# A hand-planned order: transposes, block sums, softmax subtractions and weight mixing at other places of the time table

## The chip, the cores and the metric

One core of one Trainium2 chip. The metric is device time in microseconds; the kernel before was run three times, and one further execution was taken with the hardware profiler. The work runs on five engines with a queue each: PE (TensorE: matrix products into PSUM), DVE (VectorE), ACT (ScalarE), POOL (GpSimd) and SP (SyncE, which issues the transfers). Each engine works off its queue strictly in order; an instruction whose input is not ready, or whose output buffer is not free, holds up all that stands behind it on its engine.

## The reference

Attention within chunks of 64 positions, then a product with the largest of three projections:

```python
B, H, S, D, chunk = 8, 8, 576, 64, 64
scores = scale * np.matmul(q_c, k_c.transpose(0, 1, 2, 4, 3))    # (8, 8, 9, 64, 64)
scores = scores - np.max(scores, axis=-1, keepdims=True)
attn = np.exp(scores)
attn = attn / (np.sum(attn, axis=-1, keepdims=True) + 1e-09)
out = np.matmul(attn, v_c)
x = out.transpose(0, 2, 1, 3).reshape(4608, 512)
h = np.maximum(np.maximum(x @ w1, x @ w2), x @ w3)               # each w: 512 x 768
return h @ w_out                                                 # 768 x 512
```

All of it is fp32.

## The kernel before

**Tiles and units.** The 4608 tokens are 36 tiles of 128. Eight tiles (two groups of four) go through the products plainly; the other 28 are four units of 7, 8, 7 and 6 tiles, whose products are computed by blocks with seven products in place of eight (`ORDER`, `OUTER` give their order). Each fp32 factor is split into a high and a low part, so each product is three matmuls (lines 173 to 176 for the groups, `product`, line 584, for the units).

**One tile** goes through: scores `S` (PE, L227), maximum `mx` (DVE, L232), subtraction `sub` (DVE, L237), `exp` (ACT, L241), `sum`, `eps`, `rec` (DVE, L182, L185, L188), the scaling `nrm` (L191, on DVE for the first tiles, on POOL for the later ones), the transpose `T` (PE, L253), its copy `at` (ACT, L258), the product with the values `V` (PE, L265) and the copy `x` into the staging tile (ACT, L279).

**One unit.** First its operands: sums of blocks `mix` (L496; numbers 5 and 6 on DVE, 7 and 4 on POOL), `high` parts (ACT, L501) and `low` parts (DVE, L505). Then nine sets (`hidden`: three column blocks jp by three weights w), each with the seven products of `ORDER` (1, 6, 5, 2, 7, 3, 4). Products 1, 6 and 5 are copied out of PSUM by ACT (L598) after which 2, 7 and 3 accumulate in the same banks (`banks_of_product`); DVE adds products 7, 3 and 4 to kept blocks (L601) and takes the maximum (L595), POOL adds two more (L604, L608). After the last weight of a column block seven operands Y are made for the second product: t5 and t6 on DVE (L638, L626), t7 and t4 on POOL (L638), high parts on ACT (L631), low parts on DVE (L634). Then `project` multiplies Y with w_out: copies on ACT (L675), sums on DVE (L678) and POOL (L681), stores. Block sums of the weights are made meanwhile (`store` L370 to L405, `store_out` L426 to L461).

**What sets the order.** The order of each engine's queue is written by hand. The start is a list of names, `FIRST`. From there on a planner writes it: `plan(at, pe, fn)` puts a piece of work into a heap under a due time, and each step of the PE's main work advances a clock and lets out what has come due, in the order of due times:

```python
    def passed(step):
        nonlocal now
        now += step
        while due and due[0][0] <= now:
            _, _, pe, fn = heapq.heappop(due)
            fn()
            now += pe
```

The numbers in `SOFTMAX`, in `operands_behind`, in the `after` lists of `hidden` and `project`, in `tiles` and `transposes` are such due times in us, relative to a step of PE. They change nothing but the place at which an instruction stands in its engine's queue; at run time nothing waits for them, only for data and buffers.

Of the kernel before, what the change touches and what calls it, by code (L numbers as in the profile page):

```python
# [64 lines left out]
def chunk_attn_maxout_kernel(  # L65
# [223 lines left out]
    def moe(t0, x_of, banks_in=((ps_m, "pm"),)):  # L289
# [50 lines left out]
        def project(*tts, before=JT - 1):  # L340

            for js in (range(before), range(before, JT)):
                for tt in tts:
                    for j in js:
                        onto(tt, j)
                        yield [(0.3, lambda tt=tt: output(tt))] if j == JT - 1 else []

        def hidden(j, w):
            for ct, _ in enumerate(products(j, w, 0, 512)):
                yield [] if ct < CT - 1 else [(0.3, lambda: maximum(j, w, 0, 512))] + (  # L350
                [(1.1, lambda: high(j, 0, 512)), (1.8, lambda: low(j, 0, 512))] if w == 2 else [])
# [8 lines left out]
    def store(n):  # L360
# [42 lines left out]
        def mixed():  # L403
            for k in range(2):
# [13 lines left out]
    def store_out(jp):  # L418
# [41 lines left out]
        def mixed():  # L460
# [4 lines left out]
        return [(0.0, whole(0)), (2.1, whole(1)), (3.5, originals), (4.2, sum_of(2, a21, a22, plus, True)),  # L465
                (5.9, sum_of(0, sums(2), a11, minus)), (7.6, sum_of(1, a11, a21, minus)),
                (9.3, sum_of(3, a12, sums(0), minus)), (12.0, high), (13.4, low), (17.0, mixed)]
# [3 lines left out]
    def unit(t0, count, rooms):  # L471
# [35 lines left out]
        def operands():  # L507
            return [(0.0, high(1)), (1.2, low(1)), (2.4, mix(5, b12, b11, nc.vector)), (3.4, high(5)),
                    (3.6, mix(6, b22, source[5], nc.vector)), (4.6, mix(7, b22, b12, nc.gpsimd)), (4.8, high(6)),
                    (5.8, low(6)), (5.9, high(2)), (7.0, low(5)), (8.0, mix(4, b21, source[6], nc.gpsimd)), (8.2, low(2)),  # L510
                    (8.3, high(7)), (9.4, low(7))]

        def operands_behind():

            return [(0.1, high(1)), (1.3, low(1)), (2.5, mix(5, b12, b11, nc.vector)), (2.5, mix(7, b22, b12, nc.gpsimd)),
                    (3.6, mix(6, b22, source[5], nc.vector)), (4.4, high(5)), (5.5, low(5)), (6.3, high(6)),
                    (6.7, mix(4, b21, source[6], nc.gpsimd)), (7.2, high(2)), (7.4, low(6)), (8.2, high(7)), (8.5, low(2)),
                    (9.7, low(7))]
# [68 lines left out]
        def hidden(n, loads):  # L587
# [18 lines left out]
            after = {1: [(0.25, copy(1, 0))], 5: [(0.25, copy(5, 1))],  # L606
                     6: [(0.25, copy(6, 2)),
                         (0.95, lambda: nc.gpsimd.tensor_tensor(out=kept(2), in0=kept(2), in1=kept(0), op=plus))],  # L608
                     7: [(0.25, sum_to(7, 0, lambda: kept(3))), (1.0, fourth)],
                     3: [(0.25, sum_to(3, 2, lambda: o[3] if w else M(0, 1)))],  # L610
# [3 lines left out]
            else:  # L614
                after[2] = [(0.25, greater(0, 0, lambda: o[2]))]
                after[7].append((2.2, greater(1, 1, lambda: kept(1))))
                after[3].append((0.95, greater(0, 1, lambda: o[3])))
                after[4].append((0.95, greater(1, 0, lambda: o[4])))
            if w == 2:
# [17 lines left out]
                def less(eng, out, x, y):  # L637
# [18 lines left out]
        def project(loads):  # L656
# [3 lines left out]
            def store(m, name, make):  # L660
# [11 lines left out]
                return [(0.25, fn), (1.0, out)]  # L672
# [10 lines left out]
            for p, i in enumerate(OUTER):  # L683
                for m in range(2):
                    after = {1: lambda: [(0.25, copy(m, 1, 0))],
                             2: lambda: store(m, (0, 0), lambda out, m=m: nc.scalar.copy(out=out, in_=o[m][2])),
                             6: lambda: [(0.25, copy(m, 6, 2)), (0.95, second(m))],
                             7: lambda: [(0.25, lambda m=m: sum_of(m, 7, 0)(kept(m)))],
# [3 lines left out]
                    if m:  # L692
                        after += [(0.3, fn) for fn in loads[p]]
# [145 lines left out]
    def first_tiles(time):  # L839
        gap = (time - 8.0) / 8  # L840
        for n in range(UNITS[0] + 2):
            at = now + 7.0 + gap * n
            insert(at, (("V", n - 2), ("S", n)))
            softmax(n, at, nc.vector if n < UNITS[0] else nc.gpsimd)
            if n < UNITS[0] + 1:
                insert(at + 9.2, (("T", n),))
                plan(at + 9.6, 0.0, lambda n=n: steps(n)["at"]())
            if n < UNITS[0]:
                plan(at + 0.5, 0.0, lambda n=n: steps(n)["v"]())
            if n > 1:  # L850
                plan(at + 1.0, 0.0, lambda n=n: steps(n - 2)["x"]())
# [163 lines left out]
```

## Time and profile before

| what | us |
|---|---|
| three runs | 631.44, 632.88, 632.89 (median 632.88) |
| profiled execution, whole | 632.87 |
| its span on the core | 631.1 |
| PE busy in the span | 615.1 (97%) |
| DVE, ACT, POOL busy | 445.7 (71%), 272.0 (43%), 278.6 (44%) |

Times in the trace are us from the span's start. A PE row of the timeline with xcount n is n matmuls back to back; its bracket is the idle time ahead of it and the instruction whose end released it. A group's busy time is not its time on the clock: matmuls overlap.

### The profile page before, as it was taken

To read this page: it belongs to the slowest core of one execution; us is meant where nothing else is said; L and a number is where in the kernel's file an instruction comes from. 1 tells how busy PE (TensorE), PEld (TensorE's weight loads), DVE (VectorE), ACT (ScalarE), POOL (GpSimd) and SP (SyncE) were. 2 spreads that over 40 slices of the span, in tenths; PEclk is the share of its full clock that TensorE was granted. 3 is DMA by queue.
4 is the path that set the end of the run, shared out by engine and by line. 5 is a ranking of instruction groups with operands and counts; after the bars stand their busy time and mean duration, and the time that the engine had idled before them with its cause. 6 is when DMAs were issued, how large, how long until landed. Compare 5 with 4: busy or idle time off the path is not lost.

```text
span 631.1 us, 12694 instructions
## 1 busy us (share of the span) xinstructions
PE 615.1 (97%) x5102; PEld 533.7 (85%) x5102; DVE 445.7 (71%) x684; ACT 272.0 (43%) x483; POOL 278.6 (44%) x235
## 2 busy tenths in 40 slices
PE   7899999999999999999999999989999999999997
PEld 3788887887889888888887888778999899999997
DVE  4898964788756879589559585985476758466752
ACT  4887634345544534353434342533252335232340
POOL 2422577765446864336325252352343535143430
PEclk9999999999999999999999999989999999999999
DMA  8978558575789998475967574748956756987774
GB/s 331 370 286 302 197 184 342 200 277 186 307 258 338 343 343 328 135 267 175 404 224 249 169 260 157 259 160 298 335 178 193 246 160 221 356 290 258 235 226 174
DMA packets 54220, 161.26 MB, mean 256 GB/s; under 512 B 4881, under 2 KB 17169, under 8 KB 49169
## 3 DMA queue, kind: packets, MB, share of 16 engines
q1 hardware_dynamic: 54160, 160.45, 71.8%
q8 instruction: 40, 0.66, 0.4%
q14 instruction: 20, 0.16, 0.1%
HBM read 128.97 MB, written 31.46 MB: 254 GB/s over the span
## 4 chain that ended last, share of the span: by engine, by line
PE 73%; DVE 18%; ACT 3%; issue 3%; POOL 2%; DVEq 0%; POOLq 0%; ACTq 0%
PE pm L584 52%; PE pm L174 5%; PE pm L175 5%; PE pm L176 5%; DVE Y L634 4%; DVE e L237 2%; DVE mx L232 1%; DVE sm L182 1%; PE s L265 1%; PE s L227 1%; DVE most L595 1%; DVE sm L185 1%; DVE s L391 1%; DVE X L505 1%; ACT e L241 1%
## 5 line engine op out<-in xcount | busy, mean ns | idle before, releaser
L584 PE MATMUL pm<-X,ring 128*128 128x448 f32 (+2 forms) x1512 | 313.6, 366 | 3.4 <-DVE most L601 2.0
L584 PEld LDWEIGHTS pm<-X,ring 128*128 128x128 f32 x1512 | 276.2, 188 | 31.9 <-DVE most L601 4.2
L598 ACT COPY kept<-pm 128x448 f32<-128x448 f32 (+2 forms) x108 | 57.4, 534 | 142.9 <-PE pm L584 118.6
L584 PE MATMUL pm<-Y,ring 128*128 128x448 f32 (+2 forms) x504 | 106.5, 370 | 1.0 <-DVE kept L678 0.4
L584 PEld LDWEIGHTS pm<-Y,ring 128*128 128x128 f32 x504 | 93.2, 190 | 11.4 <-DVE Y L634 1.1
L595 DVE TENSOR_TENSOR most<-pm,most 128x448 f32<-128x448 f32 (+2 forms) x72 | 44.8, 622 | 53.3 <-PE pm L584 51.9
L608 POOL TENSOR_TENSOR kept<-kept 128x448 f32<-128x448 f32 (+2 forms) x36 | 45.0, 1251 | 72.8 <-ACT kept L598 72.8
L634 DVE TENSOR_TENSOR Y<-most,Y 128x448 fp32r<-128x448 f32 (+2 forms) x72 | 58.0, 822 | 12.1 <-ACT Y L631 12.0
L174 PE MATMUL pm<-xh,wl 128*128 128x512 f32 (+1 forms) x156 | 60.8, 390 | 0.0
L175 PE MATMUL pm<-xl,wh 128*128 128x512 f32 (+1 forms) x156 | 58.4, 374 | 0.3 <-DVE xl L276 0.3
L176 PE MATMUL pm<-xh,wh 128*128 128x512 f32 (+1 forms) x156 | 58.4, 375 | 0.0
L191 POOL TENSOR_TENSOR e<-e,sm 128x512 f32<-128x512 f32 x26 | 28.7, 1104 | 61.1 <-DVE sm L188 60.2
L604 POOL TENSOR_TENSOR kept<-kept 128x448 f32<-128x448 f32 (+2 forms) x24 | 31.0, 1292 | 55.4 <-DVE kept L601 55.4
L631 ACT CAST Y<-most 128x448 fp32r<-128x448 f32 (+2 forms) x72 | 40.1, 568 | 22.4 <-DVE most L595 15.3
L601 DVE TENSOR_TENSOR kept<-pm,kept 128x448 f32<-128x448 f32 (+2 forms) x36 | 22.3, 620 | 22.2 <-PE pm L584 10.8
L241 ACT ACTIVATE e<-e 128x512 f32<-128x512 f32 x36 | 22.8, 633 | 33.6 <-DVE e L237 33.4
L601 DVE TENSOR_TENSOR pm<-pm,kept 128x448 f32<-128x448 f32 (+2 forms) x48 | 30.1, 628 | 5.6 <-PE pm L584 5.3
L176 PEld LDWEIGHTS pm<-xh,wh 128*128 128x128 f32 x156 | 29.3, 188 | 5.5
L174 PEld LDWEIGHTS pm<-xh,wl 128*128 128x128 f32 x156 | 29.3, 188 | 5.5
L175 PEld LDWEIGHTS pm<-xl,wh 128*128 128x128 f32 x156 | 29.4, 189 | 5.2 <-DVE xl L276 0.5
L232 DVE TENSOR_REDUCE mx<-s 128x8 f32<-128x512 f32 x27 | 18.4, 683 | 20.8 <-ACT stage L279 12.1
L182 DVE TENSOR_REDUCE sm<-e 128x8 f32<-128x512 f32 x36 | 24.5, 681 | 7.1 <-ACT e L241 6.6
(111 smaller groups left out, 852.2 us busy)
## 6 DMA issues: line engine op xcount, KB each, us to landing
ring<-w SPq DMA_DIRECT2D x36, 1024.0 KB, 5.2
ring<-w SPq DMA_DIRECT2D x36, 768.0 KB, 4.6
ring<-wo SPq DMA_DIRECT2D x28, 768.0 KB, 4.6
buf<-in_qk SPq DMA_DIRECT2D x36, 512.0 KB, 6.0
buf<-in_vb SPq DMA_DIRECT2D x36, 256.0 KB, 4.9
w<-s SPq DMA_DIRECT2D x18, 512.0 KB, 4.4
stage<-in_w SPq DMA_DIRECT2D x7, 512.0 KB, 4.6
out_t<-ao SPq DMA_DIRECT2D x16, 224.0 KB, 6.1
```

The costliest lines, as they stand in the source:

```text
L174: nc.tensor.matmul(out=o, lhsT=al, rhs=bh, start=first, stop=False)
L175: nc.tensor.matmul(out=o, lhsT=ah, rhs=bl, start=False, stop=False)
L176: nc.tensor.matmul(out=o, lhsT=ah, rhs=bh, start=False, stop=last)
L182: nc.vector.tensor_reduce(out=sm, in_=e, axis=AX.X, op=ALU.add)
L584: nc.tensor.matmul(out=o[i], lhsT=a, rhs=b, start=new and k == 0, stop=last and k == 2, skip_group_check=i in banks_of_product)
L595: return lambda: nc.vector.tensor_tensor(out=M(k, c), in0=of(), in1=M(k, c), op=most)
L598: return lambda: nc.scalar.copy(out=kept(k), in_=o[i])
L601: return lambda: nc.vector.tensor_tensor(out=out(), in0=o[i], in1=kept(k), op=plus)
L604: nc.gpsimd.tensor_tensor(out=kept(1) if w else M(1, 1), in0=kept(3), in1=kept(1), op=plus)
L608: (0.95, lambda: nc.gpsimd.tensor_tensor(out=kept(2), in0=kept(2), in1=kept(0), op=plus))],
L631: return lambda: nc.scalar.copy(out=y_room(i, jp)[:, 0, :half], in_=t[i]())
L634: return lambda: nc.vector.tensor_tensor(out=y_room(i, jp)[:, 1, :half], in0=t[i](), in1=y_room(i, jp)[:, 0, :half].bitcast(F32), op=minus)
```

## The change

Only the planner's numbers change. Every engine has the same instructions as before, in another order from about 95 us on. The core of the diff:

```diff
-SOFTMAX = (("mx", 1.0), ("sub", 1.9), ("exp", 2.8), ("sum", 3.8), ("eps", 4.7), ("rec", 4.9), ("nrm", 5.3))
+SOFTMAX = (("mx", 1.12), ("sub", 1.12), ("exp", 2.8), ("sum", 3.8), ("eps", 4.7), ("rec", 4.9), ("nrm", 5.3))
-OPERANDS = 0.3
-MIX = 0.5
+OPERANDS = 0.28
+MIX = 0.19
...
         def operands_behind():
-            return [(0.1, high(1)), (1.3, low(1)), (2.5, mix(5, b12, b11, nc.vector)), (2.5, mix(7, b22, b12, nc.gpsimd)),
-                    (3.6, mix(6, b22, source[5], nc.vector)), (4.4, high(5)), (5.5, low(5)), (6.3, high(6)),
-                    (6.7, mix(4, b21, source[6], nc.gpsimd)), (7.2, high(2)), (7.4, low(6)), (8.2, high(7)), (8.5, low(2)),
+            return [(0.1, high(1)), (1.25, low(1)), (2.5, mix(5, b12, b11, nc.vector)), (2.5, mix(7, b22, b12, nc.gpsimd)),
+                    (2.52, mix(6, b22, source[5], nc.vector)), (4.53, high(5)), (5.5, low(5)), (6.3, high(6)),
+                    (6.58, mix(4, b21, source[6], nc.gpsimd)), (7.48, high(2)), (6.48, low(6)), (8.2, high(7)), (9.66, low(2)),
                     (9.7, low(7))]
...
-            after = {1: [(0.25, copy(1, 0))], 5: [(0.25, copy(5, 1))],
-                     6: [(0.25, copy(6, 2)),
+            after = {1: [(0.33, copy(1, 0))], 5: [(0.69, copy(5, 1))],
+                     6: [(0.0, copy(6, 2)),
...
-                     7: [(0.25, sum_to(7, 0, lambda: kept(3))), (1.0, fourth)],
-                     3: [(0.25, sum_to(3, 2, lambda: o[3] if w else M(0, 1)))],
+                     7: [(0.11, sum_to(7, 0, lambda: kept(3))), (1.0, fourth)],
+                     3: [(0.0, sum_to(3, 2, lambda: o[3] if w else M(0, 1)))],
...
-                             (1.0, less(nc.gpsimd, t[7], lambda: M(1, 1), lambda: M(0, 1))), (1.6, t6), (1.9, high(5)),
-                             (2.6, low(5)), (3.0, high(2)), (3.6, low(2)),
+                             (1.13, less(nc.gpsimd, t[7], lambda: M(1, 1), lambda: M(0, 1))), (1.9, t6), (1.12, high(5)),
+                             (2.62, low(5)), (3.0, high(2)), (3.21, low(2)),
...
-                             (6.9 if last else 5.2 * f, high(3)), (7.5 if last else 5.9 * f, low(3)),
-                             (5.8 * f, high(7)), (6.5 * f, low(7)), (6.4 * f, high(6)), (7.1 * f, low(6)),
-                             (7.0 * f, high(4)), (7.7 * f, low(4))]
+                             (5.33 if last else 4.94 * f, high(3)), (7.5 if last else 6.07 * f, low(3)),
+                             (4.91 * f, high(7)), (6.62 * f, low(7)), (6.4 * f, high(6)), (7.46 * f, low(6)),
+                             (6.66 * f, high(4)), (7.57 * f, low(4))]
...
-                    after = {1: lambda: [(0.25, copy(m, 1, 0))],
+                    after = {1: lambda: [(0.85, copy(m, 1, 0))],
...
-                             7: lambda: [(0.25, lambda m=m: sum_of(m, 7, 0)(kept(m)))],
+                             7: lambda: [(2.0, lambda m=m: sum_of(m, 7, 0)(kept(m)))],
...
-            plan(at + 0.5, 0.0, lambda: steps(n)["at"]())
+            plan(at + 1.19, 0.0, lambda: steps(n)["at"]())
...
-                plan(at - 16.0 + 2.0 * k, 0.0, lambda n=n: steps(n)["v"]())
+                plan(at - 16.34 + 2.0 * k, 0.0, lambda n=n: steps(n)["v"]())
...
-                transposes(n, at + begin + 9.2)
+                transposes(n, at + begin + 10.83)
...
-        parts.append(("do", lambda u=u: operands(u + 1, 6.5)))
+        parts.append(("do", lambda u=u: operands(u + 1, 7.23)))
```

The sums of the weights' blocks (`store`, `store_out`), the first tiles, the loads of q and the ring's loads shift in the same way, by 0.02 to 2 us.

On PE, in the project part of the second unit (around 403 to 418 us), the first `L253` is the transpose of tile 22, the second that of tile 23, and `L265` is the values' product of tile 22. Before:

```order
L584 MATMUL pm<-Y,ring 128x512 x6
L253 MATMUL y<-ident,e 128x128 x4
L584 MATMUL pm<-Y,ring 128x512 x54
L253 MATMUL s<-ident,e 128x128 x4
L584 MATMUL pm<-Y,ring 128x512 x27
L265 MATMUL y<-xs,buf 64x64 x16
```

and now:

```order
L584 MATMUL pm<-Y,ring 128x512 x15
L253 MATMUL y<-ident,e 128x128 x4
L584 MATMUL pm<-Y,ring 128x512 x51
L253 MATMUL s<-ident,e 128x128 x4
L584 MATMUL pm<-Y,ring 128x512 x21
L265 MATMUL y<-xs,buf 64x64 x16
```

Both transposes have moved back, by nine and by six matmuls.

On POOL, at the same place, `L191` is the scaling of tile 23 and the first `L496` is mix 7:

```order
 L638 TENSOR_TENSOR most<-most 128x512
 L638 TENSOR_TENSOR most<-most,m 128x512
+L191 TENSOR_TENSOR e<-e,sm 128x512
 L496 TENSOR_TENSOR stage<-stage 128x2x448
-L191 TENSOR_TENSOR e<-e,sm 128x512
-L681 TENSOR_TENSOR kept<-kept 128x512
+L681 TENSOR_TENSOR kept<-kept 128x512 x2
 L496 TENSOR_TENSOR most<-stage,most 128x2x448
-L681 TENSOR_TENSOR kept<-kept 128x512
```

The scaling has changed places with mix 7, and mix 4 has gone behind the second sum of `project`.

On DVE, in the first unit's third set of the second column block (246 to 253 us), `L232`, `L237`, `L182`, `L185` are steps of tile 14, and the `L601` are the sums of products 7, 3 and 4. Before:

```order
L232 TENSOR_REDUCE mx<-y 128x2x4
L237 TENSOR_TENSOR e<-y,mx 128x2x4x64
L634 TENSOR_TENSOR Y<-most,Y 128x448 x2
L601 TENSOR_TENSOR kept<-pm,kept 128x448
L182 TENSOR_REDUCE sm<-e 128x8
L634 TENSOR_TENSOR Y<-m,Y 128x448
L185 TENSOR_SCALAR sm<-sm 128x8
L634 TENSOR_TENSOR Y<-most,Y 128x448
L601 TENSOR_TENSOR most<-pm,kept 128x448
L188 RECIPROCAL sm<-sm 128x8
L601 TENSOR_TENSOR most<-pm,kept 128x448
```

and now:

```order
L232 TENSOR_REDUCE mx<-y 128x2x4
L237 TENSOR_TENSOR e<-y,mx 128x2x4x64
L634 TENSOR_TENSOR Y<-most,Y 128x448
L601 TENSOR_TENSOR kept<-pm,kept 128x448
L634 TENSOR_TENSOR Y<-most,Y 128x448
L182 TENSOR_REDUCE sm<-e 128x8
L634 TENSOR_TENSOR Y<-m,Y 128x448
L601 TENSOR_TENSOR most<-pm,kept 128x448
L634 TENSOR_TENSOR Y<-most,Y 128x448
L185 TENSOR_SCALAR sm<-sm 128x8
L188 RECIPROCAL sm<-sm 128x8
L601 TENSOR_TENSOR most<-pm,kept 128x448
```

The sums of products 7 and 3 each stand one low part of Y earlier. The same two exchanges stand in the third unit (493 to 499 us).

## Rows read from the trace of the kernel before

**Rows 1.** The profile page, its first part (busy time, share of the span, instructions) and a group of its fifth part (xcount | busy, mean ns of one | idle time before them).

```profile
PE 615.1 (97%) x5102; PEld 533.7 (85%) x5102; DVE 445.7 (71%) x684; ACT 272.0 (43%) x483; POOL 278.6 (44%) x235
...
L584 PE MATMUL pm<-X,ring 128*128 128x448 f32 (+2 forms) x1512 | 313.6, 366 | 3.4 <-DVE most L601 2.0
```

**Rows 2.** Busy time by stretch (the stretch in us, its length, then for each engine the busy time with its count, PEclk, DMA share, GB/s).

```profile
0.00:27.00 27.00, 22.17 (x367) 14.31 (x367) 17.11 (x33) 16.24 (x28) 12.21 (x16) 1.00 0.91 340
...
205.00:256.00 51.00, 47.91 (x473) 42.48 (x472) 42.17 (x65) 23.54 (x44) 32.26 (x27) 1.00 0.88 320
...
620.00:631.10 11.10, 7.72 (x45) 7.40 (x43) 3.30 (x6) 0.00 (x0) 0.00 (x0) 1.00 0.30 111
```

**Rows 3.** What PE waited for from 100 us to the end: what waits <- what it waited for: us in total, times, the longest.

```profile
PE s L253 <- POOL e L191: 2.2, 1, 2.2
PE pm L584 <- DVE most L601: 2.0, 2, 1.5
PE pm L584 <- ACT kept L598: 1.2, 1, 1.2
PE pm L584 <- DVE kept L678: 0.4, 1, 0.4
PE pm L584 <- DVE Y L634: 0.4, 1, 0.4
PE s L265 <- ACT xs L258: 0.4, 1, 0.4
PE y L227 <- issue: 0.4, 1, 0.4
```

**Rows 4.** Timeline around 408 us (start, length, engine, line, operation, xcount, in brackets the idle time before and what ended it).

```profile
407.01 1.09 DVE L496 TENSOR_TENSOR most<-stage 128x896 f32<-128x896 f32 x1
408.19 2.12 POOL L496 TENSOR_TENSOR stage<-stage 128x896 f32<-128x896 f32 x1 [5.66 <-DVE sm L185]
408.22 0.20 DVE L188 RECIPROCAL sm<-sm 128x8 f32<-128x8 f32 x1
408.34 2.92 DVE L496 TENSOR_TENSOR most<-stage,most 128x896 f32<-128x896 f32 x1
410.27 1.89 POOL L191 TENSOR_TENSOR e<-e,sm 128x512 f32<-128x512 f32 x1
...
412.21 0.69 PE L253 MATMUL s<-ident,e 128*128 128x128 f32 x4 [2.23 <-POOL e L191]
```

**Rows 5.** Busy time by stretch, the five us that follow; columns as in rows 2.

```profile
412.20:417.20 5.00, 4.99 (x17) 4.03 (x18) 5.00 (x3) 2.68 (x5) 5.00 (x3) 0.66 0.18 71
```

**Rows 6.** Timeline from 214 to 225 us; columns as in rows 4.

```profile
214.65 1.23 DVE L448 TENSOR_TENSOR so<-c,so 128x1024 fp32r<-128x1024 f32 x1 [0.84 <-ACT so L445]
...
222.50 0.61 DVE L601 TENSOR_TENSOR most<-pm,kept 128x448 f32<-128x448 f32 x1
223.04 0.68 DVE L237 TENSOR_TENSOR e<-y,mx 128x512 f32<-128x512 f32 x1
223.75 0.63 ACT L241 ACTIVATE e<-e 128x512 f32<-128x512 f32 x1 [3.59 <-DVE e L237]
224.28 0.95 ACT L598 COPY kept<-pm 128x448 f32<-128x448 f32 x2
...
224.85 1.48 PE L584 MATMUL pm<-X,ring 128*128 128x448 f32 x6 [1.16 <-ACT kept L598]
```

**Rows 7.** Timeline from 248 to 253 us; columns as in rows 4.

```profile
248.73 0.62 DVE L634 TENSOR_TENSOR Y<-most,Y 128x448 fp32r<-128x448 f32 x1 [0.62 <-ACT Y L631]
...
250.40 1.29 DVE L634 TENSOR_TENSOR Y<-m,Y 128x448 fp32r<-128x448 f32 x1
251.69 0.61 DVE L634 TENSOR_TENSOR Y<-most,Y 128x448 fp32r<-128x448 f32 x1
252.23 0.61 DVE L601 TENSOR_TENSOR most<-pm,kept 128x448 f32<-128x448 f32 x1
...
252.90 1.48 PE L584 MATMUL pm<-X,ring 128*128 128x448 f32 x6 [1.46 <-DVE most L601]
```

**Rows 8.** Timeline from 274 to 296 us; columns as in rows 4.

```profile
275.88 0.57 DVE L634 TENSOR_TENSOR Y<-most,Y 128x448 fp32r<-128x448 f32 x1
276.50 3.16 PE L584 MATMUL pm<-Y,ring 128*128 128x448 f32 x14 [0.42 <-DVE Y L634]
...
291.28 3.40 DVE L505 TENSOR_TENSOR X<-stage,X 128x1024 fp32r<-128x1024 f32 x1
...
295.27 2.09 PE L584 MATMUL pm<-Y,ring 128*128 128x448 f32 x9 [0.43 <-DVE kept L678]
```

**Rows 9.** Timeline from 487 to 499 us; columns as in rows 4.

```profile
487.95 0.53 ACT L598 COPY kept<-pm 128x448 f32<-128x448 f32 x1 [3.02 <-DVE sm L185]
488.67 0.57 ACT L631 CAST Y<-most 128x448 fp32r<-128x448 f32 x1 [0.18 <-DVE most L638]
...
491.71 6.33 PE L584 MATMUL pm<-X,ring 128*128 128x448 f32 x30
...
496.41 1.58 DVE L634 TENSOR_TENSOR Y<-most,Y 128x448 fp32r<-128x448 f32 x1
497.91 1.14 DVE L601 TENSOR_TENSOR most<-pm,kept 128x448 f32<-128x448 f32 x2
498.58 1.70 PE L584 MATMUL pm<-X,ring 128*128 128x448 f32 x7 [0.53 <-DVE most L601]
```

More of the change, by code (lines that the diff above doesn't have):

```diff
@@ L350, in hidden @@
                 yield [] if ct < CT - 1 else [(0.3, lambda: maximum(j, w, 0, 512))] + (
-                [(1.1, lambda: high(j, 0, 512)), (1.8, lambda: low(j, 0, 512))] if w == 2 else [])
+                [(1.66, lambda: high(j, 0, 512)), (2.13, lambda: low(j, 0, 512))] if w == 2 else [])
         return dict(products=products, maximum=maximum, high=high, low=low, hidden=hidden, project=project, places=places,
@@ L409, in store @@
         ops[f"K{jp}{w}"] = originals
-        return [(0.0, whole(0, a)), (1.1, whole(1, b)), (2.2, sum_of(1, a21, a22, plus, True)),
-                (2.9, sum_of(0, sums(1), a11, minus)), (3.6, sum_of(2, a11, a21, minus)),
-                (4.3, sum_of(3, a12, sums(0), minus)), (5.3, high), (6.5, low), (9.2, mixed)]
+        return [(0.0, whole(0, a)), (1.1, whole(1, b)), (1.33, sum_of(1, a21, a22, plus, True)),
+                (2.4, sum_of(0, sums(1), a11, minus)), (3.6, sum_of(2, a11, a21, minus)),
+                (4.3, sum_of(3, a12, sums(0), minus)), (4.96, high), (5.63, low), (9.47, mixed)]
     place = {i: p for p, i in enumerate(ORDER)}
@@ L464, in store_out @@
         a11, a12, a21, a22 = part(0, 0), part(0, 1), part(1, 0), part(1, 1)
-        return [(0.0, whole(0)), (2.1, whole(1)), (3.5, originals), (4.2, sum_of(2, a21, a22, plus, True)),
-                (5.9, sum_of(0, sums(2), a11, minus)), (7.6, sum_of(1, a11, a21, minus)),
-                (9.3, sum_of(3, a12, sums(0), minus)), (12.0, high), (13.4, low), (17.0, mixed)]
+        return [(0.03, whole(0)), (3.03, whole(1)), (3.62, originals), (5.17, sum_of(2, a21, a22, plus, True)),
+                (5.9, sum_of(0, sums(2), a11, minus)), (7.28, sum_of(1, a11, a21, minus)),
+                (8.99, sum_of(3, a12, sums(0), minus)), (12.0, high), (13.4, low), (17.0, mixed)]
     turns = [0, 0]
@@ L670, in out @@
                     nc.sync.dma_start(out=out_t[256 * k + m * P:256 * k + (m + 1) * P, at:at + half], in_=st["o"])
-                return [(0.25, fn), (1.0, out)]
+                return [(0.25, fn), (0.82, out)]
             def copy(m, i, k):
@@ L692, in project @@
                     if m:
-                        after += [(0.3, fn) for fn in loads[p]]
+                        after += [(0.0, fn) for fn in loads[p]]
                     for jp in range(3):
@@ L841, in first_tiles @@
         for n in range(UNITS[0] + 2):
-            at = now + 7.0 + gap * n
+            at = now + 7.05 + gap * n
             insert(at, (("V", n - 2), ("S", n)))
@@ L845, in first_tiles @@
             if n < UNITS[0] + 1:
-                insert(at + 9.2, (("T", n),))
-                plan(at + 9.6, 0.0, lambda n=n: steps(n)["at"]())
+                insert(at + 8.98, (("T", n),))
+                plan(at + 9.54, 0.0, lambda n=n: steps(n)["at"]())
             if n < UNITS[0]:
@@ L850, in first_tiles @@
             if n > 1:
-                plan(at + 1.0, 0.0, lambda n=n: steps(n - 2)["x"]())
+                plan(at + 0.89, 0.0, lambda n=n: steps(n - 2)["x"]())
     pairs = []
@@ L868, in tiles @@
         nexts = own[1:] + (pairs[u][:1] if u < len(pairs) else [[]])
-        lead = 20.5 if u == 1 else 20.0
+        lead = 20.64 if u == 1 else 20.0
         gap = (time - 10.0 - lead) / (len(own) - 1)
         if u == 1:
-            transposes(own[0][1], now + 9.0)
+            transposes(own[0][1], now + 9.08)
         for i, (values, scores) in enumerate(zip(own, nexts)):
@@ L927, in stores_out @@
             for at, fn in store_out(jp):
-                plan(now + 22.0 + 17.0 * jp + at, 0.0, fn)
+                plan(now + 21.74 + 16.98 * jp + at, 0.0, fn)
     inner = 3 * JT * CT * STEP + UNITS[0] * TILE
@@ L938, in chunk_attn_maxout_kernel @@
     parts += [("steps", lambda j=j, w=w: g["hidden"](j, w)) for j in range(JT) for w in range(3)]
-    parts += [("do", change), ("do", lambda: operands(0, OPERANDS)), ("do", lambda: last_operands(0, 4 * JT * STEP + 0.1)),
+    parts += [("do", change), ("do", lambda: operands(0, OPERANDS)), ("do", lambda: last_operands(0, 4 * JT * STEP + 0.32)),
               ("do", stores_out),
-              ("do", lambda: tiles(1, 4 * JT * STEP + span(0))), ("do", lambda: load(0, 0, 0.0, 1.0)), ("do", lambda: load(0, 1, 2.0, 3.0))]
+              ("do", lambda: tiles(1, 4 * JT * STEP + span(0))), ("do", lambda: load(0, 0, 0.0, 0.98)), ("do", lambda: load(0, 1, 2.11, 3.0))]
     parts += [("steps", lambda: g["project"](0, 1)), ("steps", lambda: g["project"](2)), ("steps", lambda: g["project"](3))]
```

24 lines of the change are left out of this document (12 added, 12 removed).

## The prediction

> **What bounds the kernel now.** I read the page first, then the busy time by stretch, then the list of what PE waited for, and last the timeline around each of those waits. The page shows PE busy 615.1 of 631.1 us [rows 1], the others far less; so the end is set by PE's work and by the 16.0 us in which PE stands still, and a change of order alone can only touch those. By stretch, 4.83 us of them lie before 27 us, where nothing is moved, and 3.38 after 620 us, mostly the last store [rows 2]. What is left, about 7.8 us, lies between. The list of PE's waits names it from 100 us on [rows 3]: one wait of 2.2 for the scaling of a tile, two of 2.0 together for sums L601, one of 1.2 for a copy L598, and single ones of 0.4 for a sum L678, a low part L634, the copy of a transposed tile, and one for nothing that the profile shows.
>
> Two corrections turn idle time into lost time. A matmul's row lasts 0.366 us [rows 1], but in a run of 30 without a pause the next begins after (6.33 - 0.37) / 29 = 0.206 [rows 9]; a pause empties that overlap, so each costs its idle time and 0.16 more. And behind the longest pause the granted clock is 0.66 over 5 us [rows 5], a mixture of TensorE's two levels, 2.4 and 1.2 GHz: (1 - 0.66) x 5.0 = 1.7 us. What went before it is a stop of 2.23 us with only 0.4 us of transposes behind [rows 4]; the stop of 1.46 us left the clock of its stretch at 1.00 [rows 2, 7].
>
> **The change, part by part.** No instruction is added or taken away, so the work of each engine stays; only waits change. The profiled execution took 632.87 us, which is also the median of the runs, so the sum needs no correction.
>
> *The transpose of tile 23.* PE arrives at 412.21 - 2.23 = 409.98 and waits for the scaling L191 on POOL, which stands behind mix 7 (408.19, 2.12 us) and ends at 412.16. The chain: reciprocal on DVE until 408.42, then POOL. In the new order the scaling is ahead of mix 7, the reciprocal ahead of DVE's mix 5 (1.09 us) [rows 4], and the transpose six matmuls later. The reciprocal ends between 407.3 and 408.4, the scaling, 1.89 us long here [rows 4], at 410.3 at the latest, and PE asks at 409.98 + 6 x 0.206 = 411.2. The cover is 0.9 us at least; the wait goes whole, 2.23 + 0.16 = 2.4, and with it the slow clock, 1.7. If the cover failed by less than the 1.46 us of [rows 7], the clock would stay up all the same. Sum **4.1**. The copy of the transposed tile comes later too, but its reader, the values' product, stands 21 matmuls behind the transpose, 4.3 us.
>
> *The block sums ahead of low parts.* At 252.90 PE waited 1.46 us for the sum of product 3 (252.23, 0.61 us), which stood behind low part 4 (251.69 to 252.23, 0.54); before that DVE was idle for 0.62 waiting for a high part on ACT [rows 7], and those casts now stand earlier on ACT, so DVE can begin on low part 7 or on the sum of product 7 at once. The eps step moves behind as well, 0.07. Together 0.54 + 0.62 + 0.07 = 1.23 of the 1.46 + 0.16; some 0.25 to 0.4 stays; I take **1.35** as gained. At 498.58 the wait of 0.53 is for a sum that stood behind a low part of 1.5 us (496.41 to 497.91) [rows 9], now it stands ahead: the whole 0.53 + 0.16 = **0.7**.
>
> *Subtraction at once.* At 224.85 PE waited 1.16 us for a copy L598, queued on ACT behind the exponential, which waited for the subtraction at 223.04, which stood on DVE behind a sum L601 that begins at 222.50 [rows 6]. The subtraction now follows the maximum directly: 0.54 earlier. DVE's idle 0.84 at 214.65 [rows 6] also goes, since a low part is put in ahead of the one that waits for ACT. Here, though, the sums of products 7 and 3 stand behind two low parts, where before they were between them. Nothing in the trace shows that order; bounds are 0 (the wait only changes its name) and 1.16 + 0.16. I take **0.85**, nearer the upper end, since 0.54 + 0.84 is more than the wait.
>
> *Smaller ones.* The sum L678 that held PE 0.43 us at 295.27 stood behind a low part of 3.40 us (291.28) and is put ahead of it: 0.6. The low part at 275.88 that held PE 0.42 at 276.50 [rows 8] goes ahead of two short softmax steps: 0.45 of 0.58. The copy of the transposed tile at 157 us [rows 3] is asked for two steps of PE later: 0.55. The wait without a cause stays.
>
> *New waits.* In the third unit's operands the second sum of `project` now stands behind two low parts X, and PE comes there 4 us sooner. Before, the like exchange cost 0.43 [rows 8]; bounds are 0 and 3.4, the length of the low part; I take 0.5, by the nearest row. In ten places the first copy of a set stands behind one or two casts for Y on ACT; they begin within 0.72 us of each other now [rows 9], and a cast takes 0.57. Product 2 goes into that bank three products after the copy's source, so that is covered; 0.5 for all of it and for whatever pauses move.
>
> Sum: 4.1 + 1.35 + 0.7 + 0.85 + 0.6 + 0.45 + 0.55 = 8.6 gained, 1.0 given back: 632.87 - 7.6 = **625.3 us**. Were all of the waits of [rows 3] but the unexplained one closed, some 8 of pauses and 1.7 of clock, about 9.8 with the shorter ones that the list rounds away, it would be 623.
>
> **The rivals.**
>
> *1. DVE stays behind.* The moved sums are only early if DVE has caught up. It is busy 42.17 of the 51 us from 205 us, where PE stood still for 3.1 [rows 2], and beside a POOL instruction it is slow: the same kind of addition took 1.09 us alone and 2.92 beside mix 7 [rows 4]. With the scaling put ahead of mix 7, the scaling, mix 7 and the two sums of `project` run on POOL one behind the other, and DVE's mixes and low parts lie beside them: one more of them slowed costs 2.92 - 1.09 = 1.83. Then only the transpose, its clock and the early wait are gained, 4.1 + 0.55, and 0 to 1.83 goes back: 628.2 to 630.0, and 627.6 to 631.0 with some of the smaller terms either way. Against it: POOL's and DVE's work in that stretch is the same, only turned round. The Trainium skill has a rule on this, in "SBUF — State Buffer", section "Who interferes with whom": a DVE instruction with two inputs in SBUF and a GpSimd instruction that reads SBUF share a port pair, and the one that issues second is blocked until the other is through. The two rows agree (2.92 against 1.09). By that rule the scaling ahead of mix 7 would hold DVE's mix 5 for up to 1.89 us and the sum would be 627.2.
>
> *2. No change that can be measured.* The pauses move to the next tight place: what PE gains at one it waits at the next one, because ACT, DVE and POOL still set the pace of the unit. For it: four of the pauses lie within 205 to 300 us [rows 6 to 8]. Against: from 256 us to the end each engine but PE has room, 71% being the most [rows 1], and the 4.1 us of tile 23 stand alone. This needs 4 or more us of new waits: 631.0 to 634.8.
>
> *3. Slower.* The casts for Y 5 and 2 are now ahead of the first copy of a set on ACT. If DVE's t5 and t6, their inputs, come late, the copy waits with them, and PE, which needs its bank for product 2, with the copy. Per set the cover is about three products of six matmuls, 3.7 us, less the casts. There are some ten such sets; to lose more than the 7.6 gained and 1.9 beyond it, each would have to cost 0.95. In the trace DVE's t5 and the copy lie within 0.2 us of each other, the cast waiting 0.18 [rows 9]; DVE would have to be some 2 us later at each of them. That speaks against it: 634.8 to 638.
>
> **How the numbers follow.** The forecast (most pauses closed) 0.57, its own range 623.2 to 627.6: below are all closed, above the three terms least sure (0.85, 1.35 and the new waits) gone. Better than that 0.05; rival 1, 0.21; rival 2, 0.10; rival 3, 0.07. Range 622.6 to 630.4: from the 623 of all pauses closed, with 0.4 for the half spread of the runs, it leaves out rivals 2 and 3 and the end of rival 1. The runs of this kernel differ by 0.2%, so 0.3%, 1.9 us, is what can be told from no change. Faster by that is all below 631.0: 0.57 + 0.05 + 0.21 = 0.83; same 0.10; slower 0.07.
>
> **What would show it.** In the changed trace: no wait of L253 for L191 near 408 us and PEclk 1.00 from 400 to 432 us; PE idle in 205 to 256 us down from 3.1 to below 1.5; no wait for L601 near 495; waits from 100 us on of 2 us or less in all; a new one of about 0.5 for L678 some 8 us after the transpose. It would be wrong if waits for L678 or L598 of a microsecond or more appear at several sets (rivals 2, 3), or if L601 keeps PE waiting in the second unit as now (rival 1).

## The result and the profile after

The changed kernel takes 622.82 us (median of four runs, 621.69 to 623.18) against 632.88 before: a ratio of 0.9843, with a 95% interval of 0.9824 to 0.9862, 10.1 us less. The forecast was 625.3, within 622.6 to 630.4: the time lies 0.2 above the lower end, and below 623.2, where the forecast's own range began. The profiled execution took 622.9 us, its span is 621.1. Of the 41 executions of the kernel before in the experiments below, 32 have a mean granted clock of 0.997 and took 631.8 to 633.3 us, and 9 have 1.000 and took 629.9 to 631.2.

The page of the changed kernel, its first part:

```profile
PE 611.1 (98%) x5101; PEld 533.2 (86%) x5102; DVE 443.2 (71%) x684; ACT 271.2 (44%) x483; POOL 280.0 (45%) x235
```

PE is idle for 10.0 us in place of 16.0 [rows 1]. The same stretches as before, and two more (columns as in rows 2):

```profile
205.00:256.00 51.00, 50.55 (x513) 45.01 (x515) 42.96 (x68) 22.93 (x44) 30.42 (x29) 1.00 0.90 330
400.00:432.00 32.00, 32.00 (x269) 27.29 (x268) 25.98 (x31) 12.59 (x20) 15.06 (x8) 1.00 0.78 284
432.00:500.00 68.00, 68.00 (x517) 62.39 (x516) 44.22 (x73) 25.16 (x49) 26.94 (x22) 1.00 0.67 232
```

From 205 to 256 us PE stands still for 0.45 us, where it was 3.09 [rows 2]; from 400 to 500 us for nothing, at a full clock. All that PE waits for from 100 us on, in place of [rows 3] (the list before has one row more than is shown there, `PE pm L584 <- ACT kept L675: 0.2, 1, 0.2`, a pause near 285 us):

```profile
PE pm L584 <- ACT kept L675: 0.6, 1, 0.6
PE pm L584 <- ACT kept L598: 0.4, 1, 0.4
```

Around the transpose of tile 23 (before: rows 4):

```profile
401.58 1.04 DVE L496 TENSOR_TENSOR most<-stage 128x896 f32<-128x896 f32 x1
401.83 1.69 POOL L191 TENSOR_TENSOR e<-e,sm 128x512 f32<-128x512 f32 x1 [4.89 <-ACT kept L675]
...
402.66 1.82 DVE L496 TENSOR_TENSOR most<-stage,most 128x896 f32<-128x896 f32 x1
...
403.49 2.97 POOL L496 TENSOR_TENSOR stage<-stage 128x896 f32<-128x896 f32 x1
403.50 0.58 ACT L675 COPY kept<-pm 128x512 f32<-128x512 f32 x1
...
405.79 0.60 PE L253 MATMUL s<-ident,e 128*128 128x128 f32 x4
```

The scaling L191 runs ahead of mix 7 (403.49) and ends at 403.52, the transpose follows at 405.79 without a wait. The copy L675 on ACT (403.50) becomes important below, and so do mix 5 and mix 6 on DVE (401.58 and 402.66).

### The profile page after: what moved, and what is told of

Same layout as the page of the kernel before. It is cut to its first block, busy times and chain, and to the rows that moved or that the text cites. A ratio compares the mean times of both kernels' runs of the same rounds, so it can differ in the third digit from the quotient of the medians.

```text
span 621.1 us, 12688 instructions
## 1 busy us (share of the span) xinstructions
PE 611.1 (98%) x5101; PEld 533.2 (86%) x5102; DVE 443.2 (71%) x684; ACT 271.2 (44%) x483; POOL 280.0 (45%) x235
## 4 chain that ended last, share of the span: by engine, by line
PE 94%; DVE 4%; ACT 1%; issue 0%; DVEq 0%; ACTq 0%
PE pm L584 65%; PE pm L174 7%; PE pm L175 7%; PE pm L176 7%; PE s L265 2%; PE s L227 2%; PE tp L253 1%; PE pm L753 1%; PE y L265 1%; PE y L253 1%; PE s L253 1%; PE y L227 1%; DVE e L237 1%; DVE mx L232 0%; DVE sm L182 0%
## 5 line engine op out<-in xcount | busy, mean ns | idle before, releaser
L584 PE MATMUL pm<-X,ring 128*128 128x448 f32 (+2 forms) x1512 | 313.1, 366 | 0.4 <-ACT kept L598 0.4
L584 PEld LDWEIGHTS pm<-X,ring 128*128 128x128 f32 x1512 | 276.5, 188 | 28.1 <-ACT kept L598 1.1
L584 PE MATMUL pm<-Y,ring 128*128 128x448 f32 (+2 forms) x504 | 103.9, 365 | 0.6 <-ACT kept L675 0.6
L584 PEld LDWEIGHTS pm<-Y,ring 128*128 128x128 f32 x504 | 92.3, 188 | 9.6 <-ACT kept L675 1.0
L191 POOL TENSOR_TENSOR e<-e,sm 128x512 f32<-128x512 f32 x26 | 29.1, 1120 | 64.8 <-DVE sm L188 50.8
L634 DVE TENSOR_TENSOR Y<-most,Y 128x448 fp32r<-128x448 f32 (+2 forms) x72 | 55.3, 789 | 2.7 <-ACT Y L631 2.5
L601 DVE TENSOR_TENSOR kept<-pm,kept 128x448 f32<-128x448 f32 (+2 forms) x36 | 22.4, 621 | 25.9 <-PE pm L584 11.7
L601 DVE TENSOR_TENSOR pm<-pm,kept 128x448 f32<-128x448 f32 (+2 forms) x48 | 30.1, 628 | 7.3 <-PE pm L584 7.0
L232 DVE TENSOR_REDUCE mx<-s 128x8 f32<-128x512 f32 x27 | 18.5, 683 | 23.0 <-ACT stage L279 14.2
L182 DVE TENSOR_REDUCE sm<-e 128x8 f32<-128x512 f32 x36 | 24.5, 681 | 4.9 <-ACT e L241 4.5
```

Of the source, the lines that this page charges most:

```text
L191: eng.tensor_tensor(out=e, in0=e, in1=sm.unsqueeze(2).broadcast_to([P, 8, 64]), op=ALU.mult)
L584: nc.tensor.matmul(out=o[i], lhsT=a, rhs=b, start=new and k == 0, stop=last and k == 2, skip_group_check=i in banks_of_product)
L601: return lambda: nc.vector.tensor_tensor(out=out(), in0=o[i], in1=kept(k), op=plus)
L634: return lambda: nc.vector.tensor_tensor(out=y_room(i, jp)[:, 1, :half], in0=t[i](), in1=y_room(i, jp)[:, 0, :half].bitcast(F32), op=minus)
```

## The experiments

Times are medians; the kernel before took 632.52, 632.16 and 632.25 us in the three groups of runs (1 to 4, 5 to 8, 9 to 12). The ratios stand with their 95% intervals and are not quotients of these medians. Where a pause is named in us it is PE's idle time; by the prediction's estimate it costs about 0.16 more.

**1. The transposes alone.**

```diff
-            plan(at + 0.5, 0.0, lambda: steps(n)["at"]())
+            plan(at + 1.19, 0.0, lambda: steps(n)["at"]())
-                transposes(n, at + begin + 9.2)
+                transposes(n, at + begin + 10.83)
```

> The kernel before with only the transposes moved back (the 10.83 in tiles, the 1.19 in transposes). Theory of separate pauses: PE asks for the transpose of tile 23 about 6 matmuls (1.4 us) later, the scaling still stands behind mix 7, so that the pause of 2.4 us shrinks to about 1.0; a pause that short leaves the granted clock at 1.00, so the 1.7 to 2 us of slow clock go whole; the pauses near 223, 251, 276, 295 and 498 us stay as they were. About 629.5 us. Rival (DVE stays behind): the scaling comes later by what PE waits less, the pause stays near 2 us and the clock drops: 632 to 633.

Measured: 631.31 us, ratio 0.9992 (0.9974 to 1.0010): no change that can be told. PE's waits, two stretches of the timeline on ACT and PE, and the stretch with its clock:

```profile
PE pm L584 <- DVE most L601: 2.6, 3, 1.5
PE pm L584 <- ACT kept L675: 2.4, 2, 2.1
PE pm L584 <- ACT kept L598: 1.2, 1, 1.2
PE pm L584 <- DVE kept L678: 0.4, 1, 0.4
PE s L265 <- ACT xs L258: 0.4, 1, 0.4
```

```profile
411.06 0.94 ACT L501 CAST X<-most 128x896 fp32r<-128x896 f32 x1 [2.20 <-DVE most L496]
...
411.90 0.58 ACT L675 COPY kept<-pm 128x512 f32<-128x512 f32 x1
...
412.53 0.96 PE L584 MATMUL pm<-Y,ring 128*128 128x512 f32 x3 [2.10 <-ACT kept L675]
```

```profile
400.00:432.00 32.00, 29.90 (x246) 24.15 (x245) 26.13 (x31) 13.87 (x22) 13.42 (x7) 0.95 0.70 245
```

The transpose no longer waits, but PE stops at the same time for as long, 2.10 us, for the copy L675, which ACT works off only behind the cast of operand 6, which waits for DVE's mix 6 (idle 2.20). So two waits lay on top of each other at 412 us in the kernel before (there the copy ends at about the same time, 412.72), and the list of waits names only the one at which PE stood. The clock drops as before. My theory missed this; the rival (632 to 633) came nearer, for another reason. The wait without a cause of [rows 3] is gone here, though PE's order near it is the same; it is in none of the later traces either, so it seems to belong to that one execution.

**2. One number for the operands.**

```diff
-        parts.append(("do", lambda u=u: operands(u + 1, 6.5)))
+        parts.append(("do", lambda u=u: operands(u + 1, 7.23)))
```

> The kernel before with one number changed, operands(u + 1, 6.5) to 7.23, which puts the scaling of tile 23 ahead of mix 7 on POOL. Theory of separate pauses: the scaling starts when the reciprocal ends (408.4) and takes 1.1 to 1.9 us, PE asks at 410.0, so the pause is 0.5 us at most and the clock stays at 1.00: 4 us gained, about 628.9 us. Rival (port time): mix 5 and mix 6 on DVE are slowed beside the scaling by up to 1.8 us, the low parts come later and a wait of 1 to 2 us for the sum L678 opens near 421 us: 630 to 631.

Measured: 627.70 us, ratio 0.9938 (0.9915 to 0.9961).

```profile
405.57 1.69 POOL L191 TENSOR_TENSOR e<-e,sm 128x512 f32<-128x512 f32 x1 [5.39 <-DVE sm L188]
...
407.24 0.57 ACT L675 COPY kept<-pm 128x512 f32<-128x512 f32 x1
...
407.31 0.66 PE L253 MATMUL s<-ident,e 128*128 128x128 f32 x4
```

With the operands later, the scaling is ahead of mix 7 and the copy L675 ahead of the cast that it stood behind: the one number lifts both waits. The transpose, where it stood before, runs without a pause. 4.8 us are gained, 4.1 of them by the terms of this place; short pauses near 208, 285 and 295 us are not there either, and one of 0.37 for a scaling opens at 424 us. The theory held, and gave 1.2 us too little.

**3. The numbers of `hidden` alone** (sums ahead of low parts, casts sooner).

```diff
-                     7: [(0.25, sum_to(7, 0, lambda: kept(3))), (1.0, fourth)],
-                     3: [(0.25, sum_to(3, 2, lambda: o[3] if w else M(0, 1)))],
+                     7: [(0.11, sum_to(7, 0, lambda: kept(3))), (1.0, fourth)],
+                     3: [(0.0, sum_to(3, 2, lambda: o[3] if w else M(0, 1)))],
...
```

> The kernel before with only the numbers of hidden changed (the after lists): the sums of products 7 and 3 ahead of low parts on DVE, the casts for Y earlier on ACT. Theory of separate pauses: the pauses near 251 us (1.6) and 498 us (0.7) fall below 0.3 each, the short one near 345 goes, the one near 223 us keeps at least half; 2.5 to 3.2 us gained, 629.7 to 630.4 us, with tile 23 unchanged (2.4 and the slow clock). Rival (DVE stays behind): the waits for L601 keep their length under another name, 631.5 to 633. Rival (casts ahead of copies): new waits of PE for L598 of 0.5 us or more at several sets, 632 to 635.

Measured: 629.71 us, ratio 0.9966 (0.9953 to 0.9980). The pauses near 251, 345 and 498 us are gone, as expected; the one near 223 us, though, has grown from 1.16 to 3.33, and the one at tile 23 (412 us here) has shrunk from 2.23 to 1.5:

```profile
PE pm L584 <- ACT kept L598: 3.3, 1, 3.3
PE s L253 <- POOL e L191: 1.5, 1, 1.5
```

```profile
222.00:232.00 10.00, 6.67 (x26) 5.73 (x25) 5.70 (x11) 1.92 (x4) 6.85 (x8) 0.83 0.85 319
400.00:432.00 32.00, 30.46 (x257) 25.07 (x256) 27.52 (x34) 15.09 (x24) 13.69 (x8) 1.00 0.78 267
```

```profile
214.39 1.22 POOL L191 TENSOR_TENSOR e<-e,sm 128x512 f32<-128x512 f32 x1 [1.50 <-DVE sm L188]
...
217.66 1.54 POOL L638 TENSOR_TENSOR most<-most,m 128x448 f32<-128x448 f32 x1
...
220.66 3.28 POOL L426 TENSOR_TENSOR f<-woh,wol 128x512 f32<-128x512 f32 x2
...
221.10 1.71 DVE L634 TENSOR_TENSOR Y<-most,Y 128x448 fp32r<-128x448 f32 x1
...
223.87 0.67 DVE L237 TENSOR_TENSOR e<-y,mx 128x512 f32<-128x512 f32 x1
...
225.11 1.38 ACT L598 COPY kept<-pm 128x448 f32<-128x448 f32 x3
...
225.68 1.86 PE L584 MATMUL pm<-X,ring 128*128 128x448 f32 x4 [3.33 <-ACT kept L598]
```

The rows are to be read from the last one back: PE waits for the copy on ACT, this stands behind the exponential of the subtraction at 223.87, that behind low part 4, which took 1.71 us beside POOL's additions (220.66). Between low part 4 and the subtraction DVE runs the maximum and a sum L601. DVE has next to no idle time here from 214 us on (0.13 us); it is slow, with POOL at work beside it all the while. POOL in turn had stood idle for 1.50 us ahead of the scaling at 214.39, with t4 (L638, 217.66) queued behind. The pause of 3.33 us cost clock as well (0.83 over 10 us, 1.7 us). At tile 23, on the other hand, the clock of the stretch stays at 1.00 with the pause of 1.5; why that pause is shorter here is not shown. I had expected tile 23 unchanged and a smaller pause at 223 us: the time is in the expected range by luck, because the two misses largely cancel.

**4. The subtraction at once alone.**

```diff
-SOFTMAX = (("mx", 1.0), ("sub", 1.9), ("exp", 2.8), ("sum", 3.8), ("eps", 4.7), ("rec", 4.9), ("nrm", 5.3))
+SOFTMAX = (("mx", 1.12), ("sub", 1.12), ("exp", 2.8), ("sum", 3.8), ("eps", 4.7), ("rec", 4.9), ("nrm", 5.3))
```

> The kernel before with only the subtraction put directly behind the maximum (SOFTMAX). Theory of separate pauses: only the pause at 223 us changes, from 1.33 to about 0.8; 632.3 us, not to be told from the time before. Rival (this edit lets DVE catch up everywhere): the pauses at 251, 276, 295 shrink too, 630 us or less.

Measured: 630.92 us, ratio 0.9985 (0.9970 to 1.0001), unclear. The pause at 223 us went from 1.16 to 0.79, about as the theory had it; of the others some stayed or grew by up to 0.3, and short ones near 27, 157 and 208 us are not there.

**5. The sums, and t4 sooner on POOL.** To experiment 3 are added:

```diff
-        lead = 20.5 if u == 1 else 20.0
+        lead = 20.64 if u == 1 else 20.0
-            transposes(own[0][1], now + 9.0)
+            transposes(own[0][1], now + 9.08)
```

> The kernel of the sums alone (the after lists of hidden) and, beside them, the numbers 20.64 and 9.08 in tiles, which put the difference t4 on POOL ahead of the scaling of tile 11 and of L608 near 213 us. In the run of the sums alone PE paused 3.5 us at 222 us: a copy behind the exponential, that behind the subtraction, that behind two low parts of 0.8 and 1.7 us that lay beside POOL's additions. Theory (the order on POOL makes the low parts late): with t4 earlier the cast and the low part of Y 4 come earlier and lie beside less of POOL's work; that pause falls below 1 us and the time to about 627 us. Rival (the order of subtraction and maximum makes the exponential late): the pause stays at 3 us or more, 629.5 us.

Measured: 624.76 us, ratio 0.9891 (0.9869 to 0.9912), 5 us below experiment 3.

```profile
211.66 1.16 POOL L638 TENSOR_TENSOR most<-most,m 128x448 f32<-128x448 f32 x1 [1.15 <-DVE Y L634]
...
216.42 0.61 DVE L634 TENSOR_TENSOR Y<-most,Y 128x448 fp32r<-128x448 f32 x1
...
218.88 1.16 POOL L604 TENSOR_TENSOR most<-kept 128x448 f32<-128x448 f32 x1 [2.86 <-DVE kept L601]
...
221.53 0.95 ACT L598 COPY kept<-pm 128x448 f32<-128x448 f32 x2
```

POOL makes t4 at 211.66, in the time in which it waited for the scaling's input, is through with the next two by 216.02 and idle for 2.86 us. Low part 4 lies in that gap and takes 0.61 us; the copy comes some 3 us sooner and PE does not wait for it. SOFTMAX is as before here, so the rival falls. The gain was 2 us above what I expected. The two numbers also bring t5 on DVE, t7 on POOL and casts on ACT forward; t4 alone was not tried, so that its place is what counts is read from these rows.

**6. The change without the later transposes** (9.2 and 0.5 as before).

> The changed kernel with the transposes where they were (9.2 and 0.5). In the trace of the changed kernel the scaling of tile 23 ends 2.3 us ahead of its transpose, so that 6 matmuls (1.4 us) less leave it ahead. Theory (the scaling's and the copy's places close the pause, the transposes are cover only): no pause near 405 us; at most one of 0.3 to 0.9 near 250 us for a scaling L191, as in the run of the sums alone: 623 to 624 us. Rival (the later transposes are needed): a pause of 1 us or more at 405 us, 624.5 to 626 us.

Measured: 624.63 us, ratio 0.9885 (0.9864 to 0.9907). There is no pause at 405 us, so cover was left there, as the theory had it; the time is in the rival's range only because a pause opened elsewhere.

```profile
PE pm L584 <- DVE kept L678: 1.0, 1, 1.0
PE y L253 <- POOL e L191: 0.6, 1, 0.6
```

```profile
409.36 5.07 DVE L505 TENSOR_TENSOR X<-stage,X 128x896 fp32r<-128x896 f32 x2
...
414.35 1.27 DVE L678 TENSOR_TENSOR kept<-pm,kept 128x512 f32<-128x512 f32 x2
...
415.08 2.09 PE L584 MATMUL pm<-Y,ring 128*128 128x512 f32 x8 [1.02 <-DVE kept L678]
```

In this order both sums L678 stand behind the two low parts of X (409.36), where the changed kernel has one of them ahead. The prediction priced at 0.5 a wait for the second sum, which stands behind two low parts in the changed kernel too: it costs nothing there. Here the first stands behind them as well, and PE waits 1.0 for it.

**7. The change without the numbers of `hidden`.**

> The changed kernel with the after lists of hidden as before (sums of products 7 and 3 behind the low parts). Theory of separate pauses: those near 251 us (1.6), 498 us (0.7) and 345 us (0.3) come back, 2.6 us: 625.4 us. Rival (DVE has caught up through the other edits, the sums' places are worth nothing now): 622.8 us and no wait for L601 above 0.5.

Measured: 625.03 us, ratio 0.9898 (0.9874 to 0.9922).

```profile
PE pm L584 <- DVE most L601: 1.3, 2, 0.8
PE pm L584 <- ACT kept L675: 0.6, 1, 0.6
PE pm L584 <- DVE kept L601: 0.4, 1, 0.4
```

2.2 us of the 2.6 expected come back. Of the waits for L601 the one near 498 us is there whole (0.54), the one near 251 at half (0.75 in place of 1.46), and one of 0.4 is new.

**8. The change without the later operands** (6.5 as before).

> The changed kernel with operands(u + 1, 6.5) as before: the scaling of tile 23 behind mix 7 on POOL and the second copy L675 behind the cast of operand 6 on ACT, the transposes late. Theory (two waits lay on top of each other at 412 us, for the scaling and for the copy): the pause is there again, 2.1 to 2.3 us, now for L675, and with it the slow clock: 626.5 to 627.5 us. Rival (the late transposes suffice): a pause of 1 us or less at full clock, 623.5 to 624 us.

Measured: 626.37 us, ratio 0.9917 (0.9889 to 0.9945).

```profile
402.72 1.09 DVE L496 TENSOR_TENSOR most<-stage,most 128x896 f32<-128x896 f32 x1
402.77 3.03 POOL L496 TENSOR_TENSOR stage<-stage 128x896 f32<-128x896 f32 x1 [5.16 <-DVE most L496]
403.73 2.10 DVE L185 TENSOR_SCALAR sm<-sm 128x8 f32<-128x8 f32 x1
...
406.24 1.69 POOL L191 TENSOR_TENSOR e<-e,sm 128x512 f32<-128x512 f32 x1 [0.44 <-ACT X L501]
...
407.98 0.66 PE L253 MATMUL s<-ident,e 128*128 128x128 f32 x4 [1.36 <-POOL e L191]
```

The size nearly fits the theory, by luck, for its mechanism does not hold: the pause is 1.36 us, for the scaling and not for the copy, at full clock. Two others make up most of the rest, 1.0 for a sum L678 at 291 us and 0.8 for a load at 537 us. The scaling stands behind mix 7, which ends at 405.80, and its input comes no sooner, since the small eps step on DVE took 2.10 us beside mix 7. The copy L675 is not late this time, because mix 6 began 0.05 us ahead of mix 7 and took 1.09 us; before, it began 0.15 behind mix 7 and took 2.92 [rows 4], and cast and copy came behind it.

**9. Two copies sooner on top of the change.**

```diff
-            after = {1: [(0.33, copy(1, 0))], 5: [(0.69, copy(5, 1))],
+            after = {1: [(0.33, copy(1, 0))], 5: [(0.0, copy(5, 1))],
-                    after = {1: lambda: [(0.85, copy(m, 1, 0))],
+                    after = {1: lambda: [(0.25, copy(m, 1, 0))],
```

> The changed kernel with two copies on ACT put sooner: the copy of product 5 (L598) at 0.0 in place of 0.69, the first copy of project (L675) at 0.25 in place of 0.85, ahead of the casts that they stood behind. In the trace of the changed kernel PE paused 0.52 us at 214 us for the one and 0.79 at 271 us for the other. Theory (each pause is the work of that one place): both fall below 0.3, nothing else opens, 621.6 to 622.2 us, 10.5 to 11.2 below the time before. Rival (the casts behind them come later and open waits elsewhere): 622.8 or more.

Measured: 621.64 us, ratio 0.9843 (0.9819 to 0.9866), the interval of the change itself.

```profile
PE pm L584 <- DVE kept L601: 0.7, 1, 0.7
PE pm L584 <- DVE Y L634: 0.2, 1, 0.2
```

Both pauses fell below 0.3, and one of 0.7 for a sum opened at 219 us: PE came there sooner than DVE. The time lies in the theory's range, but it cannot be told from that of the change, and a wait did open elsewhere, as the rival had it.

**10. The change without the lead** (20.5 and 9.0 as before).

> The changed kernel with 20.5 and 9.0 in tiles as before: on POOL the difference t4 stands behind the scaling of tile 11 and behind L608 near 213 us again. Theory (the order on POOL closes the pause at 222 us, and the subtraction does not): a pause of 1.5 to 3 us there, 624.5 to 626.5 us. Rival (with the subtraction at once the order on POOL is worth nothing): no pause above 0.6 near 222 us, 622.8 us.

Measured: 626.05 us, ratio 0.9907 (0.9880 to 0.9934).

```profile
PE pm L584 <- ACT kept L598: 2.8, 1, 2.8
```

```profile
215.95 1.53 POOL L638 TENSOR_TENSOR most<-most,m 128x448 f32<-128x448 f32 x1
...
219.38 1.71 DVE L634 TENSOR_TENSOR Y<-most,Y 128x448 fp32r<-128x448 f32 x1
...
223.55 2.77 PE L584 MATMUL pm<-X,ring 128*128 128x448 f32 x8 [2.80 <-ACT kept L598]
```

t4 is late on POOL (215.95), low part 4 takes 1.71, and PE waits 2.80, although the subtraction follows the maximum at once.

**11. The change without the subtraction at once** (SOFTMAX as before).

> The changed kernel with the subtraction at 1.9 again (SOFTMAX as before). Theory: the pause at 222 us stays closed, since it stayed closed in the run of the sums with the lead, which had this SOFTMAX too; 622.8 to 623.4 us. Rival (the subtraction closes it): a pause of 0.5 to 1.3 us near 222 us, 623.4 to 624.2 us.

Measured: 622.17 us, ratio 0.9844 (0.9821 to 0.9867): the same as the change. No pause near 222 us.

**12. Four parts of the change on the kernel before**: SOFTMAX, the numbers of `hidden`, the lead, `operands(u + 1, 7.23)`.

> The kernel before with four parts of the change only: SOFTMAX, the after lists of hidden, 20.64 and 9.08 in tiles, operands(u + 1, 7.23). Theory (these close the large pauses; the rest of the change is small change): no pause at 222, 251, 408 or 498 us; what is left is 0.56 at 157 us, about 0.7 near 250 us for a scaling and up to 1.2 near 413 us for L678, as without the later transposes: 624 to 625 us. Rival (the parts only work all together): 626 us or more.

Measured: 622.12 us, ratio 0.9847 (0.9824 to 0.9871): the whole gain, 2 to 3 us better than I expected.

```profile
PE y L253 <- POOL e L191: 0.6, 1, 0.6
PE pm L584 <- DVE Y L634: 0.5, 1, 0.5
```

The transposes, the weights' sums and the numbers of `project` are not needed for it. The 1.2 us for L678 did not come, since here one L678 stands ahead of the last two low parts. The parts overlap: experiment 2 gains 4.8 us and experiment 5 7.4, together they would be 12.2, and here, with the subtraction, it is 10.1.

## Why the prediction was right, and where it was not

*The bound* was right: only PE's pauses moved, and nearly all of them closed. Before, PE was idle for 7.8 us between 27 and 620 us; now it is 1.3 there (10.0 less 8.7 in the first 27 and the last 11 us, where it was 8.2 before). Idle time fell by 6.0 in all, the clock gave 1.7; a pause takes 0.16 more of PE's pace, for some eight pauses 1.3; that is 9.0 of the 10.0 us between the profiled executions, and 1 us is not assigned. Part of it may belong to the clock: the executions of the kernel before at 1.000 are 2.3 us shorter than the others (medians 630.21 and 632.56), where the trace gives 1.7; no trace of one was kept. *The ceiling* of 623 was none: the kernel is at 622.8 with 1.3 us of new waits left in it, and the prediction gave a time below 623.2 a chance of only 0.05.

*Tile 23*, 4.1: the pause and the slow clock of this place (2.4 and 1.7) went whole. But the reason was only half of it. I had the scaling in the way; experiment 1 shows a second wait, of 2.10 us there, under it, for the copy L675 behind a cast on ACT. The new order lifts it too, which I had not looked for. The transposes themselves, which I counted as cover, are not what closed the pause: alone they gain nothing (1), and without them it stays closed (6, 12). One number closes it, the operands' start (2); without that number it is 1.36 at full clock (8), and the sums alone leave 1.5 at full clock (3), so the other parts take some of it off as well.

*Block sums ahead of low parts*, 1.35 + 0.7: right, and slightly under. The pauses were 1.46 + 0.16 and 0.53 + 0.16 and went whole with the sums alone (3); with the sums taken away (7) the second comes back whole and the first at half, so the other parts close half of it too.

*Subtraction at once*, 0.85: this step failed. The pause at 223 us closed, but not by the subtraction: alone it takes 0.4 off (4), and without it the pause is closed as well (11). The two numbers of the lead decide (3, 5, 10), and by the rows it is t4's place on POOL, of which the prediction did not speak. The step followed the wait back through ACT to the subtraction on DVE and stopped there; DVE itself was late because its low parts lay beside POOL's additions, and these could be moved into a gap of POOL. Without that edit this pause grows, to 3.3 us with the sums alone (3) and to 2.8 us with the rest of the change (10).

*New waits*, 1.0: nearly right in sum by luck, wrong in place. Priced were 0.5 for L678 (nothing came) and 0.5 for the copies behind casts; measured are 0.64 + 0.36, each with 0.16 more, 1.3 us, all of it copies behind casts on ACT.

*What was missing* are the pauses that the list rounds away or that I left as they were (near 221, 285, 345 us, the one without a cause), some 1.4 us with the 0.16 of each. The terms set too low are another 0.9 (0.47 at 223, 0.27 at 251, 0.13 at 276 us). Less 0.3 for the new waits and 0.5 more idle time at the two ends, 1.5 of the 2.5 us between the forecast and the result have a place; the rest is the 1 us that is not assigned.

*Rival 1* (DVE stays behind) did not come true for the whole, yet its mechanism is what experiments 3 and 10 run into: low part 4 takes 1.71 us beside POOL's additions and 0.61 alone (5). The Trainium skill, "SBUF — State Buffer", section "Who interferes with whom", says that a DVE instruction with two inputs in SBUF and a GpSimd instruction that reads it exclude one another; the rows agree. The 1.89 us that I drew from this rule for the swap at tile 23 did not come: mix 5 began 0.25 us ahead of the scaling and took 1.04 us in the changed kernel, and mix 6, begun while the scaling ran, took 1.82, less than the 2.92 beside mix 7 before.

*Rival 2* and *rival 3* are out: the two waits for copies stay below a microsecond.

## What to carry to other kernels

A list of waits names for each pause only what the engine waited for at that instruction; before a pause is put down to it, look up what else the waiting engine needed at that time, and take the first cause away in an experiment to see whether a second lies under it. When one engine is full and the others fill its pauses, parts of a re-ordering don't add up: one number (the operands' start) lifted two waits, another part (the sums) made a pause longer until a third edit on another engine's queue was there. Follow a late instruction back through its whole queue, and ask of each one ahead of it that is slower than elsewhere what ran beside it.

## What the runs showed of the hardware

In the profiled executions the granted clock stayed at 1.00 in the stretches with pauses of 1.46 [rows 2, 7], 1.5 (experiment 3 at 412 us) and 1.53 us (5), and fell after pauses of 2.10 (1), 2.23 [rows 4], 2.80 (10) and 3.33 us (3); each fall cost about 1.7 us beside the pause. It does not fall in every execution of the same kernel, as the 9 of 41 under the result show.

A DVE step of 8 elements per partition, eps, took 2.10 us while POOL ran mix 7 (8) and 0.17 in the kernel before at 408.02 us, so even the smallest step of a chain can hold it up. In the 14 traces eps took more than 0.3 us 133 times, and each time an instruction of POOL was running when it began.

Of two additions that lie side by side the one that begins second is the slower here: mix 6 on DVE took 2.92 us and mix 7 on POOL 2.12 where mix 7 began 0.15 us ahead [rows 4], and 1.09 and 3.03 us where mix 6 began 0.05 ahead (8).
